# The first half of u's token contraction as filler inside attention, with w2 loaded early into the exp buffers and recalibrated scheduler costs

## Chip, cores, metric

One core of a Trainium2 chip runs the whole program. The metric is the device time of one execution in microseconds. Most executions of one kernel agree within about 1% here; each run also reports the mean granted clock of TensorE, as a share of full speed (0.972 in the profiled run of the kernel before). Engines: PE is TensorE, PEld its weight loads, DVE VectorE, ACT ScalarE, POOL GpSimd, SP SyncE.

## The reference

Four residual blocks on x (2048 tokens, 512 channels, bf16): attention, token-mixing MLP, and the same two again with the same weights.

```python
def _A_ref(x, wqkv, wo):            # 32 heads of 16, causal, window of 256 tokens
    q, k, v = ...
    scores = einsum(q, k) * Dh ** -0.5, masked
    return (softmax(scores) @ v) @ wo
def _B_ref(x, w1, b1, w2, b2):      # mixes tokens, not channels
    h = _layernorm(x)
    u = gelu(einsum("bsd,sf->bdf", h, w1) + b1)     # s = 2048 tokens, f = 1792
    return transpose(einsum("bdf,fs->bds", u, w2) + b2)
x = x + _A_ref(_layernorm(x)); x = x + _B_ref(_layernorm(x))
x = x + _A_ref(_layernorm(x)); x = x + _B_ref(_layernorm(x))
```

What matters: u contracts over tokens. Its first 8 token tiles are final when half of the query chunks of the attention are done, the last only at its end.

## The kernel before

A list scheduler on the host orders all operations of the five engines from estimated costs and latencies; the emitted program is static. On PE, scores come first ("sc"), then P·V or filler ("f": projections, output projection, y).

Shortened; "..." marks cuts, and the comments are mine.

```python
def op(self, eng, fn, ..., cost=100.0, lat=60.0, ...)     # lat=160 given for matmuls
...
w1b = sb("w1b", [P, 2, NT, 256]); w2b = sb("w2b", [P, 2, NFT, 256])    # NT = 16, NFT = 14
psum2 = Pool("psum2", 3)            # pairs of banks: scores, u
psum = Pool("psum", 2); psum.classes = {"od": [0, 1], "f": [0, 2]}     # P.V and fillers
...
def u_phase(w1t):
    last_sc = prev_sc[0]                              # the last scores of this attention
    ...
    for fb in range(NFT // 2):
        tu, tw = Tile(psum2), w1t[fb]
        for tt in range(2):
            for s0 in range(0, NT, 4):                # four token tiles at a time
                def f_u(e, ...): ...                  # 4 matmuls of 512 columns, PSUM accumulates over 16
                op("tensor", f_u, reads=[tw] + [f"xh{sc}" ...], writes=[(tu, tt)], after=[last_sc], cls="f")
        for tt in range(2):                           # gelu straight from PSUM
            op("scalar", lambda e: e.activation(uT[:, ft, :], PS[...], ACTF.Gelu_apprx_tanh, bias=b1col[...]))
...
for layer in range(2):
    prepare(0, True)                                  # layer 1: y blocks 0..3, layernorm, qkv
    for c in range(2 * NC):                           # eight query chunks
        tos[c] = attention(c, tqs, tks)               # scores, exp on ACT, mask on DVE, P.V
        if c == 5: late = [prev_sc[0]]
        if c % 2 == 0 and c // 2 + 1 < NC: prepare(c // 2 + 1, False)
        wo_block(c, tos[c], c == 2 * NC - 1)          # output projection, residual, layernorm
    w1t = [load_w1(fb, late) for fb in range(NFT // 2)]
    w2t = [load_w2(i, late) for i in range(NT // 2)]
    u_phase(w1t)
for t in range(NT): y_block(t, w2t, True); store(t)
```

The softmax here doesn't subtract the row's maximum and nothing guards it: scores larger than these inputs give would overflow.

## Time and profile before

The time is 563.89 us, median of three runs (563.68 to 564.19). The profiled run has a span of 560.8 us. I cut it into four stages. The borders are read from the times of the 304 exp instructions (152 per attention: 12 in the first query chunk, 20 in each other) and of the gelus in the trace. "Chunks" below count from 0.

| stage | before, us |
|---|---|
| A: start to the last exp of the first attention | 185.4 |
| B: from there to the last gelu | 59.1 |
| C: from there to the last exp of the second attention (y runs inside) | 207.2 |
| D: from there to the end (u again, then y) | 109.1 |

From the page of the kernel before: total busy times, then the busy share in tenths for 40 equal slices of 14.0 us, and last the granted clock in tenths.

```profile
PE 466.9 (83%) x7500; PEld 236.5 (42%) x7584; DVE 306.9 (55%) x659; ACT 342.4 (61%) x464; POOL 152.4 (27%) x266
...
PE   4967878877766969999888888999786596999997
...
ACT  0699999999988311110798997099979931120000
...
PEclk9999999999967989999999999999999998999999
```

ACT is at 9 through most of the first attention, then nearly idle in B, where PE is at 9: one engine after the other. PEclk is not at 9 in slices 11, 12 and 14, counted from 0, and once more near the end.

Stretches of the first attention in the kernel before; the columns are length, busy time with the number of instructions for each engine, granted clock, DMA share and GB/s.

```profile
core 0: us, PE busy (x) PEld busy (x) DVE busy (x) ACT busy (x) POOL busy (x), PEclk, DMA share, GB/s
91.00:147.00 56.00, 43.26 (x1154) 24.60 (x1157) 41.71 (x81) 54.96 (x74) 21.32 (x30) 1.00 0.20 52
147.00:157.00 10.00, 7.65 (x199) 3.83 (x199) 9.19 (x23) 9.45 (x14) 3.10 (x8) 1.00 0.50 123
157.00:167.40 10.40, 7.37 (x163) 3.99 (x164) 3.64 (x10) 9.80 (x14) 0.00 (x0) 0.51 0.01 2
167.40:174.30 6.90, 4.17 (x126) 2.05 (x128) 5.84 (x13) 5.67 (x9) 1.48 (x4) 0.99 0.01 2
174.30:184.50 10.20, 7.19 (x148) 4.03 (x150) 2.95 (x6) 8.60 (x13) 0.00 (x0) 0.50 0.02 4
```

Up to 147 us ACT is the bound (54.96 of 56.00) and PE has holes (43.26). From 157 us the clock is half for 10 us, full for 7, half again for 10.

The chain of waits of the kernel before in stage B: start, length, engine, what, line; L713 is u.

```profile
198.38 1.92 PE PS L713 x8
200.31 6.03 DMA w1b<-in_B_w_dram
206.38 5.88 PE PS L713 x14
212.31 10.74 PE PS L713 x49
```

Its PE timeline around the wait for a w1 block; the brackets hold the idle time and what ended it.

```profile
198.38 3.63 PE L713 MATMUL PS<-xh_sb,w1b 128*128 128x512 bf16 x16 [0.86 <-DVE xh_sb L468]
206.38 7.39 PE L713 MATMUL PS<-xh_sb,w1b 128*128 128x512 bf16 x20 [4.38 <-DMA w1b<-in_B_w_dram]
```

49 u matmuls take 10.74 us, 0.219 each (0.216 from start to start; the 10.74 hold the whole last one). After 4.38 us of idling for w1 the next 14 take 5.88 us (chain), 0.42 each: the half clock (0.50) stands in the trace for 6.8 us, from 205.0 us on. This is the "cold restart" below.

Groups of the kernel before that give durations for the additions of the change: line, engine, operation, operands, shapes, count | busy us, mean ns | idle before.

```profile
L681 DVE TENSOR_TENSOR x_sb<-x_sb,PS 128x512 bf16<-128x512 bf16 x32 | 21.8, 684 | 9.5 <-PE PS L678 9.4
...
L721 ACT ACTIVATE uT<-PS,b1col 128x512 bf16<-128x512 f32 x28 | 19.3, 688 | 83.0 <-PE PS L713 83.0
```

### The profile page before, as it was taken

To read this page: it belongs to the slowest core of one execution; us is meant where nothing else is said; L and a number is where in the kernel's file an instruction comes from. 1 tells how busy PE (TensorE), PEld (TensorE's weight loads), DVE (VectorE), ACT (ScalarE), POOL (GpSimd) and SP (SyncE) were. 2 spreads that over 40 slices of the span, in tenths; PEclk is the share of its full clock that TensorE was granted. 3 is DMA by queue.
4 is the path that set the end of the run, shared out by engine and by line. 5 is a ranking of instruction groups with operands and counts; after the bars stand their busy time and mean duration, and the time that the engine had idled before them with its cause. 6 is when DMAs were issued, how large, how long until landed. Compare 5 with 4: busy or idle time off the path is not lost.

```text
span 560.8 us, 16670 instructions
## 1 busy us (share of the span) xinstructions
PE 466.9 (83%) x7500; PEld 236.5 (42%) x7584; DVE 306.9 (55%) x659; ACT 342.4 (61%) x464; POOL 152.4 (27%) x266
## 2 busy tenths in 40 slices
PE   4967878877766969999888888999786596999997
PEld 1544444444433424445445444444444342444443
DVE  5998876886745300027866785876777630001222
ACT  0699999999988311110798997099979931120000
POOL 3874363252311000004516321651442100000000
PEclk9999999999967989999999999999999998999999
DMA  8221100002900062503312004301290005432653
GB/s 275 37 40 31 40 2 3 4 2 58 228 4 2 1 151 77 148 26 106 85 31 59 4 2 86 85 12 12 58 248 2 3 1 150 122 105 80 182 176 107
DMA packets 81367, 39.88 MB, mean 71 GB/s; under 512 B 17808, under 2 KB 81296, under 8 KB 81296
## 3 DMA queue, kind: packets, MB, share of 16 engines
q1 hardware_dynamic: 81296, 38.81, 26.7%
q8 instruction: 59, 0.97, 0.7%
q14 instruction: 12, 0.10, 0.1%
HBM read 33.56 MB, written 2.10 MB: 64 GB/s over the span
## 4 chain that ended last, share of the span: by engine, by line
PE 49%; ACT 20%; DVE 18%; POOL 5%; DMA 4%; issue 3%; POOLq 0%
ACT pt L621 18%; PE PS L713 16%; PE PS L728 15%; PE PS L647 7%; PE PS L526 4%; DVE stats L455 3%; DVE pt L631 3%; PE PS L607 3%; DVE xh_sb L468 2%; DMA w1b<-in_B_w_dram 2%; DVE x_sb L681 2%; POOL rstd L466 2%; PE PS L551 2%; DVE stg L560 2%; PE PS L678 1%
## 5 line engine op out<-in xcount | busy, mean ns | idle before, releaser
L621 ACT ACTIVATE pt<-PS 128x1024 bf16<-128x1024 f32 (+1 forms) x304 | 293.7, 1037 | 62.2 <-PE PS L607 62.1
L713 PE MATMUL PS<-xh_sb,w1b 128*128 128x512 bf16 x436 | 102.5, 392 | 11.5 <-DMA w1b<-in_B_w_dram 8.5
L728 PE MATMUL PS<-uT,w2b 128*128 128x512 bf16 x425 | 99.7, 379 | 6.1 <-issue 2.2
L647 PE MATMUL PS<-pt,vbd 128*32 128x64 bf16 (+3 forms) x1920 | 84.0, 240 | 19.6 <-DVE stg L560 5.3
L732 DVE SCALAR_TENSOR_TENSOR x_sb<-PS,b2col,x_sb 128x512 bf16<-128x512 f32 x32 | 24.0, 750 | 137.9 <-PE PS L728 137.8
L631 DVE TENSOR_TENSOR pt<-pt,ldm 128x512 bf16<-128x512 bf16 (+1 forms) x192 | 78.7, 413 | 34.8 <-ACT pt L621 33.4
L647 PE MATMUL PS<-pt,onesbd 128*32 128x64 bf16 (+3 forms) x1920 | 82.7, 238 | 0.8 <-issue 0.8
L607 PE MATMUL PS<-qT,kbd 32*128 32x64 bf16 (+3 forms) x1920 | 62.1, 236 | 18.8 <-ACT pt L621 17.3
L713 PEld LDWEIGHTS PS<-xh_sb,w1b 128*128 128x128 bf16 x448 | 44.2, 101 | 67.6 <-DMA w1b<-in_B_w_dram 9.5
L526 PE MATMUL PS<-xhT,wqkv 128*128 128x512 bf16 x227 | 61.5, 389 | 12.2 <-DVE stg L534 3.7
L721 ACT ACTIVATE uT<-PS,b1col 128x512 bf16<-128x512 f32 x28 | 19.3, 688 | 83.0 <-PE PS L713 83.0
L464 POOL TENSOR_SCALAR rstd<-agg 128x1 f32<-128x1 f32 x64 | 13.4, 209 | 206.8 <-DVE agg L457 205.2
L647 PEld LDWEIGHTS PS<-pt,vbd 128*32 128x32 bf16 x1920 | 45.1, 98 | 53.1 <-DVE oT L669 11.0
L537 POOL TENSOR_SCALAR kbd<-stg,par 128x512 bf16<-128x512 bf16 x64 | 51.6, 815 | 51.7 <-DVE stg L534 47.0
L728 PEld LDWEIGHTS PS<-uT,w2b 128*128 128x128 bf16 x448 | 41.0, 98 | 53.6 <-DVE x_sb L732 3.2
L563 POOL TENSOR_SCALAR vbd<-stg,half 128x512 bf16<-128x512 bf16 x64 | 49.4, 783 | 48.0 <-DVE stg L560 36.1
L607 PEld LDWEIGHTS PS<-qT,kbd 32*128 32x128 bf16 x1920 | 28.2, 94 | 66.7 <-ACT pt L621 44.8
L647 PEld LDWEIGHTS PS<-pt,onesbd 128*32 128x32 bf16 x1920 | 46.5, 99 | 1.2 <-issue 0.9
L455 DVE BATCH_NORM_STATS2 stats<-x_sb 128x6 f32<-128x512 bf16 x64 | 43.4, 683 | 0.9 <-DMA x_sb<-in_A_x_dram 0.3
L551 PE MATMUL PS<-wqkv,xhT 128*64 128x256 bf16 x512 | 35.3, 276 | 4.7 <-DVE stg L560 1.7
L466 POOL TENSOR_TENSOR rstd<-rstd,mhalf 128x1 f32<-128x1 f32 x64 | 37.3, 585 | 4.0
L664 ACT ACTIVATE rl<-PS 128x256 f32<-128x256 f32 x64 | 25.7, 401 | 20.0 <-PE PS L647 19.8
(36 smaller groups left out, 316.0 us busy)
## 6 DMA issues: line engine op xcount, KB each, us to landing
w1b<-in_B_w_dram SPq DMA_DIRECT2D x14, 1024.0 KB, 5.9
w2b<-in_B_w_dram SPq DMA_DIRECT2D x16, 896.0 KB, 5.4
out_dram<-x_sb SPq DMA_DIRECT2D x16, 128.0 KB, 2.2
wqkv<-in_A_wqkv_dram SPq DMA_DIRECT2D x3, 512.0 KB, 6.5
x_sb<-in_A_x_dram SPq DMA_DIRECT2D x3, 512.0 KB, 9.2
x_sb<-in_A_x_dram SPq DMA_DIRECT2D x2, 256.0 KB, 3.0
wo_sb<-in_A_wo_dram SPq DMA_DIRECT2D x1, 512.0 KB, 9.2
xhT<-xh_sb SPq DMA_TRANSPOSE x24, 2.5
```

The lines of the kernel that those rows point to most:

```text
L455: op("vector", lambda e: e.bn_stats(stats[:, t, :], x_sb[:, t, :]), reads=[f"x{t}"], writes=[f"st{t}"], cost=dve_cost(512))
L466: op("gpsimd", lambda e: e.tensor_tensor(rstd[:, t, :], rstd[:, t, :], mhalf[:], op=ALU.pow), reads=[f"rs{t}", "mhalf"], writes=[f"rs{t}"] ...
L526: mm_group(ft, 4, lambda e, c: e.matmul(bank(ft), lhsT=wqkv[:, c, which * 512 + o * P:which * 512 + (o + 1) * P], rhs=xhT[:, tx.slot, c, : ...
L537: op("gpsimd", lambda e, h=h: e.tensor_scalar(kbd[:, tk.slot, o, :, h, :], stg[:, ts.slot, :].rearrange("p (s n) -> p s n", n=64), par[:, ...
L551: last = e.matmul(bank(ft)[64 * hf:64 * hf + 64, sc * 256:(sc + 1) * 256], lhsT=xhT[:, tx.slot, c, tok:tok + 64], rhs=wqkv[:, c, 1024:1536 ...
L563: op("gpsimd", lambda e, h=h: e.tensor_scalar(vbd[:, tk.slot, 2 * sp:2 * sp + 2, :, 16 * h:16 * h + 16], stg[:, ts.slot, :].rearrange("p ( ...
L607: last = e.matmul(PS[:, 2 * tt[r // 2].slot + r % 2, base + c0 * 64:base + (c0 + n) * 64], lhsT=kbd[32 * r:32 * r + 32, tk.slot, o, jj, :, ...
L621: op("scalar", lambda e, ts=ts, tp=tp, i=i, cols=cols: e.activation(pt[:, tp.slot, 2 * i:2 * i + 2, 0:cols], PS[:, 2 * ts.slot:2 * ts.slot ...
L631: return e.tensor_tensor(v, v, msk.unsqueeze(1).to_broadcast([P, 4, w]), op=ALU.mult)
L647: last = e.matmul(bank(t)[32 * r:32 * r + 32, den * 256 + q0 * 64:den * 256 + (q0 + n) * 64], lhsT=onesbd[:] if den else vbd[:, tk.slot, j ...
L713: last = e.matmul(PS[:, 2 * tu.slot + tt, :], lhsT=w1b[:, tw.slot, sc, tt * P:(tt + 1) * P], rhs=xh_sb[:, sc, :], start=(sc == 0), stop=(s ...
L728: mm_group(ft, NFT, lambda e, fc: e.matmul(bank(ft), lhsT=w2b[:, tw.slot, fc, k * P:(k + 1) * P], rhs=uT[:, fc, :], start=(fc == 0), stop= ...
```

## The change

The intent: PE has holes while ACT computes exps (busy 43.26 of 56.00 us from 91 to 147), and ACT has little to do while PE computes u (busy 6.39 of 38.00 us from 206 to 244). So the token tiles 0 to 7 of u are contracted inside attention's second half as the lowest-ranked filler, and the f32 partial sums (28 KB per partition) lie in buffers that are free then: w2's and uT's. After attention only tiles 8 to 15 are contracted; DVE adds the partial sum into the small buffer of the softmax denominators, and ACT takes gelu from there. w1 is loaded in halves, into four buffers of half the size, and asked for two query chunks earlier. As w2's buffers are taken, the first three pairs of w2 go to the six exp buffers, which are free between the attentions. The scheduler's latencies and costs are recalibrated too.

```diff
+    LAT = {"tensor": 205.0, "vector": 125.0, "scalar": 155.0, "gpsimd": 95.0, "sync": 0.0}
     (replaces lat=60, and lat=160 for matmuls; DMA completion 1500 -> 1900; several costs of POOL and DVE)
-        w1b = sb("w1b", [P, 2, NT, 256])
-        w2b = sb("w2b", [P, 2, NFT, 256])
+        w1b = sb("w1b", [P, 4, NT // 2, 256])
+        w2b = sb("w2b", [P, 2, 4096])
...
+        def u_first(fb, tw):
+            for tt in range(2):
+                ft = filler(False)
+                dst, keys = uA(2 * fb + tt)               # f32 view of w2b or uT
+                mm_group(ft, 8, lambda e, sc, tt=tt, ft=ft: e.matmul(
+                    bank(ft), lhsT=w1b[:, tw.slot, sc, tt * P:(tt + 1) * P], rhs=xh_sb[:, sc, :],
+                    start=(sc == 0), stop=(sc == 7)), [tw] + [f"xh{sc}" for sc in range(8)],
+                    prio=1e9 + len(g.ops), after=g.users_of(keys))
+                op("vector", lambda e, dst=dst, ft=ft: e.tensor_copy(dst, bank(ft)), ...)
+        def u_second(fb, tw):
+            ...                                           # token tiles 8..15, after the last scores
+                op("vector", lambda e, ...: e.tensor_tensor(tmp(), PS[...], src, op=ALU.add), ...)
+                op("scalar", lambda e, ...: e.activation(uT[:, ft, :], tmp(), ACTF.Gelu_apprx_tanh, ...))
...
-                if c == 5:
+                if c == 3:
                     late = [prev_sc[0]]
...
+                if c == 4:
+                    for fb in range(NFT // 2):
+                        u_first(fb, load_w1(fb, 0, late))
...
+            w1t = [load_w1(fb, 1, late) for fb in range(NFT // 2)]
+            for i in range(3):
+                load_w2(i, [prev_sc[0]])                  # i < 3: into pt, two buffers for each pair
+            for fb in range(NFT // 2):
+                u_second(fb, w1t[fb])
+            load_w2(3, late)
+            load_w2(4, late)
```

More of the change, by code (lines that the diff above doesn't have):

```diff
@@ L53, in __init__, with op @@
         self.readers = {}
-    def op(self, eng, fn, reads=(), writes=(), cost=100.0, lat=60.0, prio=None, dma=False, after=(), holds=(),
+    def op(self, eng, fn, reads=(), writes=(), cost=100.0, lat=None, prio=None, dma=False, after=(), holds=(),
            cfg=None, cls=None):
         o = Op()
-        o.idx, o.eng, o.fn, o.cost, o.lat, o.dma = len(self.ops), eng, fn, cost, lat, dma
+        o.idx, o.eng, o.fn, o.cost, o.dma = len(self.ops), eng, fn, cost, dma
+        o.lat = self.LAT[eng] if lat is None else lat
         o.prio = prio
@@ L94, in op, with users_of @@
         return o
+    def users_of(self, keys):
+        return [o for k in keys for o in [self.last_w.get(k), *self.readers.get(k, ())] if o is not None]
     def _alloc_time(self, o):
@@ L187, in schedule @@
                 o.end = dma_free
-                o.done = dma_free + 1500.0
+                o.done = dma_free + 1900.0
             else:
@@ L295, in pool_cost @@
 def pool_cost(n, ptrs=0):
-    return 300 + n / 1.4 + 83 * ptrs
+    return 195 + n / 1.4 + 83 * ptrs
 def stepped(v, n, step):
@@ L386, in bass_interleave_layers__sliding_block__mixer_token_mlp__prompt_kernel @@
         p_kv, p_pt, p_rl, p_oT = Pool("kv", 3), Pool("pt", NPT), Pool("rl", 2), Pool("oT", 3)
-        p_w1, p_w2 = Pool("w1", 2), Pool("w2", 2)
+        p_w1 = Pool("w1", 4)
         op("gpsimd", lambda e: e.memset(ident[:], 1.0), writes=["ident"], cost=150)
@@ L464, in ln_block @@
             op("gpsimd", lambda e: e.tensor_scalar(rstd[:, t, :], agg[:, t, 1:2], a, b, op0=ALU.mult, op1=ALU.add),
-               reads=[f"ag{t}"], writes=[f"rs{t}"], cost=200, prio=-1e5)
+               reads=[f"ag{t}"], writes=[f"rs{t}"], cost=272, prio=-1e5)
             op("gpsimd", lambda e: e.tensor_tensor(rstd[:, t, :], rstd[:, t, :], mhalf[:], op=ALU.pow),
-               reads=[f"rs{t}", "mhalf"], writes=[f"rs{t}"], cost=350, prio=-1e5)
+               reads=[f"rs{t}", "mhalf"], writes=[f"rs{t}"], cost=520, prio=-1e5)
             op("vector", lambda e: e.tensor_scalar(xh_sb[:, t, :], x_sb[:, t, :], agg[:, t, 0:1], rstd[:, t, :],
@@ L492, in mm_group @@
                 rd = reads(k0, k1) if callable(reads) else reads
-                op("tensor", f, reads=rd, writes=[dst], cost=mm_cost(k1 - k0, cols), lat=160, prio=prio, holds=holds, after=after, cfg="f",
+                op("tensor", f, reads=rd, writes=[dst], cost=mm_cost(k1 - k0, cols), prio=prio, holds=holds, after=after, cfg="f",
                    cls="f")
@@ L514, in f_tr @@
                     return last
-                op("tensor", f_tr, reads=[f"xh{t}", "ident"], writes=[ft], cost=4 * 60, lat=160, prio=fprio(),
+                op("tensor", f_tr, reads=[f"xh{t}", "ident"], writes=[ft], cost=4 * 60, prio=fprio(),
                    holds=[tx], cfg="f", cls="f")
@@ L519, in qkv @@
                     bank(ft).bitcast(dt.bfloat16)[:, 0:512].rearrange("p (c n) -> p c n", c=4)),
-                   reads=[ft], writes=[(tx, i)], cost=dve_cost(512, psum=True), prio=-2e5)
+                   reads=[ft], writes=[(tx, i)], cost=dve_cost(512, 0.5, psum=True), prio=-2e5)
             XT = [(tx, i) for i in range(4)]
@@ L557, in f_v @@
                         return last
-                    op("tensor", f_v, reads=[(tx, sp), "w2"], writes=[ft], cost=mm_cost(4, 256), lat=160,
+                    op("tensor", f_v, reads=[(tx, sp), "w2"], writes=[ft], cost=mm_cost(4, 256),
                        prio=fprio(), holds=[ts, tk], cfg="v", cls="f")
@@ L617, in attention @@
                             rd += [(tk, "k", o, h) for h in range(2)]
-                    prev_sc[0] = op("tensor", f_sc, reads=rd, writes=[tA, tB], cost=cols / 2.4 + 15, lat=160,
+                    prev_sc[0] = op("tensor", f_sc, reads=rd, writes=[tA, tB], cost=cols / 2.4 + 15,
                                     prio=len(g.ops), after=[prev_sc[0]] if prev_sc[0] else [], cfg="sc", cls="sc")
@@ L634, in f_mask @@
                                                    op=ALU.mult)
-                        op("vector", f_mask, reads=keys + LD, writes=keys, cost=dve_cost(4 * n * nc_ * 64, 0.5) + 60)
+                        op("vector", f_mask, reads=keys + LD, writes=keys, cost=dve_cost(4 * n * nc_ * 64, 0.5))
                     for k, o, base in su:
@@ L657, in attention @@
                             rd += [(tk, "v", jj, h) for h in range(2)]
-                        op("tensor", f_pv, reads=keys + rd, writes=[od[o]], cost=plan[k][2] * 128 / 2.4 + 15, lat=160,
+                        op("tensor", f_pv, reads=keys + rd, writes=[od[o]], cost=plan[k][2] * 128 / 2.4 + 15,
                            holds=[to], prio=len(g.ops), cfg="pv", cls="pv")
@@ L686, in bass_interleave_layers__sliding_block__mixer_token_mlp__prompt_kernel, with load_w1 @@
         w2v = B_w2.rearrange("(fc p) s -> p fc s", p=P)
-        def load_w1(fb, late):
+        def load_w1(fb, hf, late):
             tw = Tile(p_w1)
-            op("sync", lambda e: e.dma_start(w1b[:, tw.slot], w1v[:, :, fb * 256:(fb + 1) * 256]), writes=[tw], dma=True,
-               cost=5000, prio=1e6 + len(g.ops), after=late)
+            op("sync", lambda e: e.dma_start(w1b[:, tw.slot], w1v[:, 8 * hf:8 * hf + 8, fb * 256:(fb + 1) * 256]),
+               writes=[tw], dma=True, cost=2500, prio=1e6 + len(g.ops), after=late)
@@ L692, in load_w1 @@
             return tw
+        w2keys = lambda i: [("w2b", 4 * (i % 2) + k) for k in range(4)]
         def load_w2(i, late):
-            tw = Tile(p_w2)
-            op("sync", lambda e: e.dma_start(w2b[:, tw.slot], w2v[:, :, i * 256:(i + 1) * 256]), writes=[tw], dma=True,
-               cost=4500, prio=1e6 + len(g.ops), after=late)
-            return tw
-        u_ops = []
-        def u_phase(w1t):
-            last_sc = prev_sc[0]
-            op("scalar", lambda e: e.preload_act_table_set("gelu_apprx_tanh_and_others"), writes=["acttab"], cost=1280)
-            for fb in range(NFT // 2):
-                tu, tw = Tile(psum2), w1t[fb]
-                prio = fprio()
-                for tt in range(2):
-                    for s0 in range(0, NT, 4):
-                        def f_u(e, s0=s0, tw=tw, tt=tt, tu=tu):
-                            last = None
-                            for sc in range(s0, s0 + 4):
-                                last = e.matmul(PS[:, 2 * tu.slot + tt, :], lhsT=w1b[:, tw.slot, sc, tt * P:(tt + 1) * P],
-                                                rhs=xh_sb[:, sc, :], start=(sc == 0), stop=(sc == NT - 1))
-                            return last
-                        u_op = op("tensor", f_u, reads=[tw] + [f"xh{sc}" for sc in range(s0, s0 + 4)], writes=[(tu, tt)],
-                           cost=mm_cost(4, 512), lat=160, prio=prio, after=[last_sc], cfg="f", cls="f")
-                        u_ops.append(u_op)
-                for tt in range(2):
-                    ft = 2 * fb + tt
-                    op("scalar", lambda e, ft=ft, tu=tu, tt=tt: e.activation(
-                        uT[:, ft, :], PS[:, 2 * tu.slot + tt, :], ACTF.Gelu_apprx_tanh, bias=b1col[:, ft:ft + 1], scale=1.0),
-                       reads=[(tu, tt), "b1", "acttab"], writes=[f"uT{ft}"], cost=act_cost(512, 1))
@@ L725, in y_block @@
-        def y_block(t, w2t, wide):
+            if i < 3:
+                halves = [Tile(p_pt), Tile(p_pt)]
+                for h, tw in enumerate(halves):
+                    op("sync", lambda e, h=h, tw=tw: e.dma_start(
+                        pt[:, tw.slot].rearrange("p a b -> p (a b)")[:, 0:NFT * 128].rearrange("p (f n) -> p f n", n=256),
+                        w2v[:, 7 * h:7 * h + 7, i * 256:(i + 1) * 256]), writes=[tw], dma=True, cost=2300,
+                       prio=1e6 + len(g.ops), after=late)
+                w2t[i] = ([[tw] for tw in halves], lambda fc: pt[:, halves[fc // 7].slot].rearrange(
+                    "p a b -> p (a b)")[:, (fc % 7) * 256:(fc % 7 + 1) * 256])
+                return
@@ new lines, in load_w2, with uA @@
+            op("sync", lambda e: e.dma_start(w2b[:, i % 2, 0:NFT * 256].rearrange("p (f n) -> p f n", n=256),
+                                             w2v[:, :, i * 256:(i + 1) * 256]), writes=w2keys(i), dma=True,
+               cost=4600, prio=1e6 + len(g.ops), after=late)
+            w2t[i] = ([w2keys(i)] * 2, lambda fc: w2b[:, i % 2, fc * 256:(fc + 1) * 256])
+        def uA(ft):
+            i = ft // 2
+            if ft % 2 == 0:
+                return (w2b[:].rearrange("p a b -> p (a b)").bitcast(dt.float32)[:, i * 512:(i + 1) * 512],
+                        [("w2b", i)])
+            return (uT[:].rearrange("p a b -> p (a b)").bitcast(dt.float32)[:, i * 512:(i + 1) * 512],
+                    [f"uT{2 * i}", f"uT{2 * i + 1}"])
@@ new lines, in bass_interleave_layers__sliding_block__mixer_token_mlp__prompt_kernel @@
+        u_ops, w2t = [], {}
+        def u_first(fb, tw):
[4 more added lines that the diff above has]
+                    bank(ft), lhsT=w1b[:, tw.slot, sc, tt * P:(tt + 1) * P], rhs=xh_sb[:, sc, :],
+                    start=(sc == 0), stop=(sc == 7)), [tw] + [f"xh{sc}" for sc in range(8)], prio=1e9 + len(g.ops),
+                    after=g.users_of(keys))
+                op("vector", lambda e, dst=dst, ft=ft: e.tensor_copy(dst, bank(ft)), reads=[ft], writes=keys,
+                   cost=dve_cost(512, psum=True), prio=-2e5)
@@ new lines, in u_second, with f_u @@
+        def u_second(fb, tw):
+            tu = Tile(psum2)
+            for s0, s1 in ((8, 12), (12, 14), (14, 16)):
+                for tt in range(2):
+                    def f_u(e, s0=s0, s1=s1, tt=tt):
+                        last = None
+                        for sc in range(s0, s1):
+                            last = e.matmul(PS[:, 2 * tu.slot + tt, :], lhsT=w1b[:, tw.slot, sc - 8, tt * P:(tt + 1) * P],
+                                            rhs=xh_sb[:, sc, :], start=(sc == 8), stop=(sc == NT - 1))
+                        return last
+                    u_ops.append(op("tensor", f_u, reads=[tw] + [f"xh{sc}" for sc in range(s0, s1)], writes=[(tu, tt)],
+                                    cost=mm_cost(s1 - s0, 512), prio=fprio(), after=[prev_sc[0]], cfg="f", cls="f"))
+            tmps = []
+            for tt in range(2):
+                src, keys = uA(2 * fb + tt)
+                tr = Tile(p_rl)
+                tmps.append((tr, lambda tr=tr: rl[:, tr.slot].rearrange("p a b -> p (a b)")))
+                op("vector", lambda e, tt=tt, src=src, tmp=tmps[tt][1]: e.tensor_tensor(
+                    tmp(), PS[:, 2 * tu.slot + tt, :], src, op=ALU.add),
+                   reads=[(tu, tt), "acttab"] + keys, writes=[tr], cost=dve_cost(512, psum=True))
+            for tt in range(2):
+                ft = 2 * fb + tt
+                tr, tmp = tmps[tt]
+                op("scalar", lambda e, ft=ft, tmp=tmp: e.activation(uT[:, ft, :], tmp(), ACTF.Gelu_apprx_tanh,
+                                                                    bias=b1col[:, ft:ft + 1], scale=1.0),
+                   reads=[tr, "b1", "acttab"], writes=[f"uT{ft}"], cost=act_cost(512, 1, psum=False))
@@ L726, in y_block @@
+        def y_block(t, wide):
+            if t % 2 == 0 and 8 <= t < NT - 2:
+                load_w2(t // 2 + 1, [])
             ft = filler(wide)
-            tw, k = w2t[t // 2], t % 2
+            k = t % 2
+            keys, w = w2t[t // 2]
             mm_group(ft, NFT, lambda e, fc: e.matmul(
-                bank(ft), lhsT=w2b[:, tw.slot, fc, k * P:(k + 1) * P], rhs=uT[:, fc, :],
+                bank(ft), lhsT=w(fc)[:, k * P:(k + 1) * P], rhs=uT[:, fc, :],
                 start=(fc == 0), stop=(fc == NFT - 1)),
-                lambda a, b: [tw] + [f"uT{fc}" for fc in range(a, b)], after=[u_ops[-8]])
+                lambda a, b: [q for h in range(a // 7, (b - 1) // 7 + 1) for q in keys[h]] +
+                             [f"uT{fc}" for fc in range(a, b)], after=u_ops[-6:-5])
@@ L736, in bass_interleave_layers__sliding_block__mixer_token_mlp__prompt_kernel @@
         out_v = out.rearrange("b (t p) d -> p (b t) d", p=P)
-        w2t = None
         for layer in range(2):
@@ L744, in prepare @@
                     if layer:
-                        y_block(t, w2t, wide)
+                        y_block(t, wide)
                     ln_block(t, False)
@@ L755, in bass_interleave_layers__sliding_block__mixer_token_mlp__prompt_kernel @@
                 wo_block(c, tos[c], c == 2 * NC - 1)
-            w1t = [load_w1(fb, late) for fb in range(NFT // 2)]
-            w2t = [load_w2(i, late) for i in range(NT // 2)]
-            u_phase(w1t)
+                if c == 4:
+                    for fb in range(NFT // 2):
+                        u_first(fb, load_w1(fb, 0, late))
+            op("scalar", lambda e: e.preload_act_table_set("gelu_apprx_tanh_and_others"), writes=["acttab"], cost=1280)
+            w1t = [load_w1(fb, 1, late) for fb in range(NFT // 2)]
[5 more added lines that the diff above has]
+            load_w2(4, late)
         for t in range(NT):
-            y_block(t, w2t, True)
+            y_block(t, True)
             op("sync", lambda e, t=t: e.dma_start(out_v[:, t, :], x_sb[:, t, :]), reads=[f"x{t}"], dma=True, cost=600,
```

## The prediction

> **What bounds it now** (slice table, stretch-by-stretch busy times; PE TensorE, ACT ScalarE, DVE VectorE).
> - Layer-1 attention is ACT-bound: in 91 to 147 us ACT is busy 55.0 of 56, PE 43.3. In 112 to 183, ACT 66.0 of 71, PE 51.6: 19 us of PE holes. From 154 to 182 the granted clock is only 0.50 to 0.95.
> - After each attention comes a serial PE tail, from the first u matmul to the last: 183.2 to 243.8 (60.6 us), 449.6 to 507.9 (58.4 us). The chain of waits there is almost only u matmuls: 224 at 0.219 us (49 in 10.74 us), 49.1 us. The rest is output projection, end of P·V, a 0.9 us wait for xh, a 4.4 or 4.2 us idle wait for a w1 load, and a slow restart: 14 matmuls in 5.88 us instead of 3.1 (4.56 in the second tail). [...]
> - y with layer-2 attention (244 to 413): PE 150 of 169; final y: 48 of 53, PE-bound.
>
> **What the change does.** PE's work stays. The instruction order shows only 56 (layer 1) and 44 (layer 2) of the 112 first-half u matmuls before attention's last output projection; 56 and 68 follow it and fill the wait for the last layernorm, where 40 u matmuls stood before anyway. From the last score matmuls on, the new tail holds 178 and 190 u matmuls, 39.1 and 41.7 us, plus 4 to 5 us of projection and P·V and 2 to 3 us of softmax latency: about 46 and 49 us against 61 and 59. The w1 wait and cold restart should vanish: first halves are loaded during attention, second halves in half-size loads. Gain about 15 + 10 = 25 us.
>
> Added: 28 DVE copies and 28 additions of 128x512 f32 (estimate 0.69 us each, from the 0.684 us of the PSUM copies and residual additions): 39 us. About half the copies fall in attention (DVE busy 47 of 71); the additions fall where DVE idles (0 busy in 206 to 244) and delay gelu by a microsecond. ACT and DMA bytes unchanged.
>
> **Given back.** 46 and 40 more matmuls (10 and 9 us) enter fragmented PE holes of 19 and 12 us; each pair delays a score matmul by up to 0.44 us. I expect 2 us lost per layer. The w2 prefetch fills all six exp buffers at the start of layer-2 attention and queues ahead of second-half w1 loads: 1 us. The recalibrated scheduler constants reorder everything; taken as neutral to slightly good.
>
> **Prediction: 542 us**, 8 in 10 within 533 to 553. Faster by over 2%: 0.88; within 2%: 0.11; slower: 0.01.
>
> **What would show it.**
> - From the last score matmuls to the last u matmul: 44 to 51 us per layer, without a w1 wait over 1 us.
> - Attention's second half (fourth to eighth query chunk) within 3 us per layer of before.
> - DVE busy up by 35 to 42 us; PE busy within 10 us.
> - y's first matmuls wait under 1.5 us for gelu.
>
> **What would make it wrong.** Filler delaying scores so that ACT loses over 3 us per layer; second-half w1 loads stuck behind the w2 prefetch; layer-2 exps waiting for buffers held by w2. On the other side, a fuller PE keeping the clock up from 154 to 189 us, or better constants removing small DVE waits, would bring it under 535.

(25 us gained, less 2 per layer and 1, make 20; 542 us lies 22 below the time.)

## More of the kernel before

Over the 10 us ahead of the first fall PE was busy 7.65, about as large a share as in the stretch up to 147 us. But in the last 3.4 us ahead of each of the two falls it was busy for only 1.89 and 1.23 us:

```profile
153.80:157.20 3.40, 1.89 (x75) 1.00 (x64) 3.37 (x10) 3.40 (x6) 1.62 (x4) 1.00 0.02 5
170.90:174.30 3.40, 1.23 (x52) 0.73 (x56) 2.73 (x8) 3.40 (x6) 1.39 (x4) 1.00 0.00 0
```

## The result, and the profile after

The changed kernel takes 527.13 us (median of four runs, 527.03 to 528.50) against 563.78 us (560.69 to 564.19) in the same series; the ratio is 0.9367, 95% interval 0.9330 to 0.9403. Ratios here are the mean of one kernel's fast runs over the mean of the other's in the same rounds, so not quite the ratio of the medians. The gain is 36.7 us; 22 were predicted, and 527 lies below the stated range of 533 to 553.

| stage | before | after | change | predicted change |
|---|---|---|---|---|
| A: to the last exp of the first attention | 185.4 | 178.5 | -6.9 | +2 |
| B: to the last gelu | 59.1 | 44.5 | -14.6 | -15 |
| C: to the last exp of the second attention | 207.2 | 203.6 | -3.6 | +3 |
| D: to the end | 109.1 | 98.7 | -10.4 | -10 |
| sum (profiled runs) | 560.8 | 525.3 | -35.5 | -20 |

(The prediction's figures are put to the stages here: the 1 us for the w2 prefetch is counted in C. They add up to 20 us, near the 22 that it took off the time.) B and D came as predicted. The surplus is in A, 8.9 us, and in C, 6.7.

C needs a closer look, which the times of the instructions in the traces allow. First, the last gelu comes later after the last u matmul than before, as the addition stands between them; measured to the first y matmul instead, B went from 58.0 to 41.8 us and C from 208.3 to 206.2, so about 1.6 us of C's surplus belong to B. Second, the second attention itself did not get shorter: from its first exp to its last it took 182.5 us before and 183.8 after. What shrank is the start of C, from the last gelu to the first exp, 24.7 us before and 19.7 after, with 70 y matmuls ahead of that exp instead of 80.

The same lines of the page, for the changed kernel; a slice is now 13.1 us.

```profile
PE 455.1 (87%) x7495; PEld 234.0 (45%) x7584; DVE 340.0 (65%) x715; ACT 340.1 (65%) x464; POOL 150.7 (29%) x266
...
PE   4977788878888899999988888999787889998997
...
ACT  0589999999999703403996997079999960231000
...
PEclk9989999999999999999999999999999999999999
```

PEclk shows one small dip at the start (half clock for 3.41 us, from 30.7 us on), and 9 from there on. DVE busy rose by 33 us.

Stretches of the changed kernel: chunk 6 to the last exp, and stage B in two parts.

```profile
core 0: us, PE busy (x) PEld busy (x) DVE busy (x) ACT busy (x) POOL busy (x), PEclk, DMA share, GB/s
137.40:178.50 41.10, 34.99 (x839) 18.19 (x846) 29.01 (x66) 41.10 (x57) 8.33 (x16) 1.00 0.13 36
178.50:202.00 23.50, 22.16 (x161) 10.69 (x163) 12.14 (x23) 3.45 (x7) 1.49 (x4) 1.00 0.84 224
202.00:223.00 21.00, 20.89 (x97) 9.51 (x97) 7.73 (x12) 8.28 (x13) 0.00 (x0) 1.00 0.42 121
```

From 137.4 to 178.5 us ACT is busy 41.10 of 41.10 us: no hole is left at the bound, with u filler on PE that was not there before. The same stretch of the kernel before, chunk 6 to the last exp:

```profile
138.50:185.40 46.90, 33.70 (x819) 18.35 (x820) 28.24 (x63) 42.55 (x57) 7.63 (x16) 0.78 0.33 82
```

It lasted 46.9 us, with ACT busy 42.55, at a mean clock of 0.78. So 5.8 of A's 6.9 us lie here. What ACT waited for from chunk 5 to the last exp (engine, line, releaser: us in total, times, longest), before and after:

```profile
ACT pt L621 <- PE PS L607: 3.0, 7, 1.2
ACT rl L664 <- PE PS L647: 1.9, 4, 0.8
```

```profile
ACT pt L628 <- PE PS L614: 0.5, 2, 0.3
ACT rl L671 <- PE PS L654: 0.2, 1, 0.2
```

The chain of waits of the changed kernel in stage B; L738 is the first half of u, L752 the second, L685 the output projection; the first line is the last of attention's work.

```profile
182.76 1.73 PE PS L685 x8
184.49 7.34 PE PS L738 x34
191.88 4.70 PE PS L738 x21
196.57 6.04 PE PS L752 x28
202.67 10.74 PE PS L752 x49
```

No wait for w1 and no cold stretch is left (the clock is 1.00 in both parts of stage B): 34 + 21 first-half matmuls cover the last layernorm, and the second half follows at 0.219 us each. The durations of the additions:

```profile
L768 ACT ACTIVATE uT<-rl,b1col 128x512 bf16<-128x512 f32 x28 | 18.7, 714 | 70.0 <-DVE rl L762 70.0
...
L762 DVE TENSOR_TENSOR rl<-PS,w2b 128x512 f32<-128x512 f32 x14 | 9.7, 692 | 31.5 <-PE PS L752 31.5
L742 DVE COPY w2b<-PS 128x512 f32<-128x512 f32 x14 | 9.7, 690 | 8.0 <-PE PS L738 8.0
```

They are as estimated: 0.69 us for a copy and for an addition. Gelu from SBUF takes 714 ns, from PSUM 688.

One odd thing is in the second layer's tail. PE timeline of the changed kernel there:

```profile
465.70 5.56 PE L752 MATMUL PS<-xh_sb,w1b 128*128 128x512 bf16 x25
471.10 5.34 PE L778 MATMUL PS<-uT,pt 128*128 128x512 bf16 x23
476.28 1.03 PE L738 MATMUL PS<-xh_sb,w1b 128*128 128x512 bf16 x4
478.82 8.38 PE L778 MATMUL PS<-uT,pt 128*128 128x512 bf16 x37 [1.51 <-DVE rl L762]
```

Four first-half matmuls (L738) run only after 23 matmuls of y (L778), and then PE waits 1.51 us for the addition that needed them. They rank below the second half and y. Below, they are called the straggler.

### The profile page after: what moved, and what is told of

The parts are those of the page before. It is cut to its first block, busy times and chain, and to the rows that moved or that the text cites. A ratio compares the mean times of both kernels' runs of the same rounds, so it can differ in the third digit from the quotient of the medians.

```text
span 525.3 us, 16776 instructions
## 1 busy us (share of the span) xinstructions
PE 455.1 (87%) x7495; PEld 234.0 (45%) x7584; DVE 340.0 (65%) x715; ACT 340.1 (65%) x464; POOL 150.7 (29%) x266
## 4 chain that ended last, share of the span: by engine, by line
PE 46%; ACT 34%; DVE 16%; issue 1%; DMA 1%; POOL 1%
ACT pt L628 30%; PE PS L778 16%; PE PS L752 9%; PE PS L738 7%; PE PS L654 5%; PE PS L533 3%; DVE stats L462 3%; PE PS L558 2%; DVE pt L638 2%; ACT rl L671 2%; PE PS L614 2%; DVE xh_sb L475 2%; DVE stg L567 2%; ACT rl L673 2%; PE PS L685 2%
## 5 line engine op out<-in xcount | busy, mean ns | idle before, releaser
L628 ACT ACTIVATE pt<-PS 128x1024 bf16<-128x1024 f32 (+1 forms) x304 | 297.9, 1075 | 60.3 <-PE PS L614 58.7
L654 PE MATMUL PS<-pt,vbd 128*32 128x64 bf16 (+3 forms) x1920 | 80.6, 235 | 13.5 <-DVE stg L541 5.1
L654 PE MATMUL PS<-pt,onesbd 128*32 128x64 bf16 (+3 forms) x1920 | 78.6, 233 | 0.0
L778 PE MATMUL PS<-uT,w2b 128*128 128x512 bf16 x263 | 61.6, 379 | 3.5 <-issue 2.1
L768 ACT ACTIVATE uT<-rl,b1col 128x512 bf16<-128x512 f32 x28 | 18.7, 714 | 70.0 <-DVE rl L762 70.0
L654 PEld LDWEIGHTS PS<-pt,vbd 128*32 128x32 bf16 x1920 | 44.5, 96 | 42.9 <-DVE oT L676 10.9
L544 POOL TENSOR_SCALAR kbd<-stg,par 128x512 bf16<-128x512 bf16 x64 | 49.7, 786 | 47.8 <-DVE stg L541 46.9
L738 PE MATMUL PS<-xh_sb,w1b 128*128 128x512 bf16 x209 | 50.1, 380 | 7.0 <-DVE w2b L742 2.4
L752 PE MATMUL PS<-xh_sb,w1b 128*128 128x512 bf16 x220 | 48.5, 379 | 0.2
L778 PE MATMUL PS<-uT,pt 128*128 128x512 bf16 x162 | 37.5, 379 | 2.6 <-DVE rl L762 1.5
L778 PEld LDWEIGHTS PS<-uT,w2b 128*128 128x128 bf16 x280 | 25.4, 98 | 32.0 <-DVE x_sb L688 0.9
L685 PE MATMUL PS<-wo_sb,oT 128*128 128x512 bf16 x112 | 30.5, 381 | 10.5 <-DVE x_sb L688 5.1
```

Of the source, the lines that this page charges most:

```text
L544: op("gpsimd", lambda e, h=h: e.tensor_scalar(kbd[:, tk.slot, o, :, h, :], stg[:, ts.slot, :].rearrange("p (s n) -> p s n", n=64), par[:, ...
L628: op("scalar", lambda e, ts=ts, tp=tp, i=i, cols=cols: e.activation(pt[:, tp.slot, 2 * i:2 * i + 2, 0:cols], PS[:, 2 * ts.slot:2 * ts.slot ...
L654: last = e.matmul(bank(t)[32 * r:32 * r + 32, den * 256 + q0 * 64:den * 256 + (q0 + n) * 64], lhsT=onesbd[:] if den else vbd[:, tk.slot, j ...
L738: mm_group(ft, 8, lambda e, sc, tt=tt, ft=ft: e.matmul(bank(ft), lhsT=w1b[:, tw.slot, sc, tt * P:(tt + 1) * P], rhs=xh_sb[:, sc, :], start ...
L752: last = e.matmul(PS[:, 2 * tu.slot + tt, :], lhsT=w1b[:, tw.slot, sc - 8, tt * P:(tt + 1) * P], rhs=xh_sb[:, sc, :], start=(sc == 8), sto ...
L778: mm_group(ft, NFT, lambda e, fc: e.matmul(bank(ft), lhsT=w(fc)[:, k * P:(k + 1) * P], rhs=uT[:, fc, :], start=(fc == 0), stop=(fc == NFT ...
```

## The experiments

Twelve runs. The question is why stages A and C, the attentions, became shorter although they took in more PE work. Theory A is that the recalibrated constants give better orders. Theory B is that the filler itself does it, by keeping the TensorE clock up where it had fallen. All kernels gave correct results. The first four ran together on one chip, the next four on a second, the last four on a third.

### e1_constants: only the constants

```diff
 kernel before
-    lat=60.0 (and lat=160 for matmuls), dma_free + 1500.0, 300 + n / 1.4, ...
+    LAT = {"tensor": 205.0, "vector": 125.0, ...}, dma_free + 1900.0, 195 + n / 1.4, ...   (all as in the change)
```

> The kernel before with only the scheduler's recalibrated latencies and costs; u, w1 and w2 as before. The open question is 15 us more gain than predicted, 10 of them in the second halves of the two attentions (5.5 and 4.1 us shorter although they took in 56 and 44 more matmuls). Theory A, the constants: about 553 us (551 to 556), the second halves (fourth chunk's end to the last exp) 5 and 4 us shorter, ACT without waits on scores there. Theory B, the filler matmuls themselves, which keep the TensorE clock at 1.0 from 154 to 189 us: 560 to 565 us, the clock still dips in that stretch, the second halves as before.

Measured: 549.82 us (547.39 to 554.04), ratio 0.9763 (0.9702 to 0.9823). That is more gain than either theory said (whether it exceeds 2% is unclear by the interval), and only partly where theory A put it: from chunk 4 to the last exp the first attention became 3.4 us shorter, the second 0.6 longer. Stages A to D changed by -4.6, -4.6, -2.5 and -3.4 us. Chunk 6 to the last exp became 43.3 us, and the clock there still falls, to a mean of 0.85.

The spread of the runs goes with the clock: 547.39 us at a mean clock of 0.984, 554.04 at 0.969. The tails shrink in part because the new order does the output projection in one piece and waits 5.3 us for w1 in place of 8.5.

### e2_structure: everything but the constants

```diff
 changed kernel
-    LAT = {"tensor": 205.0, "vector": 125.0, "scalar": 155.0, "gpsimd": 95.0, "sync": 0.0}, ...
+    LAT = {"tensor": 160.0, "vector": 60.0, "scalar": 60.0, "gpsimd": 60.0, "sync": 60.0}, ... (all as before)
```

> The changed kernel with the old latencies and costs in the scheduler. Theory A (constants): 536 to 540 us, the second halves of the attentions 4 to 5 us longer than in the changed kernel, ACT again waiting on scores. Theory B (filler keeps the clock up): 526 to 531 us, clock near 1.0 in the first attention's second half.

Measured: 527.62 us (527.24 to 527.69), ratio 0.9359: the same as the changed kernel. Theory A, as an explanation of the surplus in the total, falls here: with the structure in place the constants are worth nothing net. The stages differ, though. A is 180.8 us here (178.5 with the new constants), C is 206.2 (203.6), and D is 94.0 (98.7): the old constants put more u matmuls into the second attention and leave no straggler, which pays for the longer A and C. So within A and C the constants do have a part of the surplus, 2.3 and 2.6 us. Chunk 6 to the last exp has full clock with the old constants as well (1.00), and ACT is busy 41.47 of its 41.70 us.

### e3_dummy: only useless filler

```diff
 kernel before
                 wo_block(c, tos[c], c == 2 * NC - 1)
+                if c == 4 and layer == 0:
+                    for n in range(7):
+                        ft = filler(False)
+                        mm_group(ft, 8, lambda e, sc, ft=ft: e.matmul(
+                            bank(ft), lhsT=wo_sb[:, sc % 4, 0:P], rhs=xh_sb[:, sc, :], ...),   # never read
+                            ["wo"] + [f"xh{sc}" for sc in range(8)], prio=1e9 + len(g.ops))
```

> The kernel before with 56 useless 512-column matmuls (results never read, so outputs stay right) as lowest-priority filler in the second half of the first attention, at the places where the changed kernel does its u matmuls; everything else as before, old constants, and 12.3 us more PE work in all. Theory B: the granted clock stays near 1.0 there, that half is 3 to 6 us shorter, and the total falls to 556 to 561 us in spite of the added work. Theory A: no shorter, 564 to 568 us.

Measured: 553.82 us (552.83 to 555.97), ratio 0.9831 (0.9784 to 0.9877). With 56 matmuls that nobody reads, 12.3 us of PE work at 0.2195 us each, the program became about 10 us faster (faster beyond doubt, whether by 2% is unclear by the interval). The clock does not fall there (1.00), and chunk 6 to the last exp takes 42.3 us in place of 46.9:

```profile
139.40:181.70 42.30, 36.99 (x860) 19.81 (x871) 27.25 (x62) 41.43 (x57) 7.76 (x16) 1.00 0.37 92
```

Stage B shrank too, by 6.0 us. Eight of the useless matmuls stand where PE had waited for w1 (197.19 us), but the order of the useful instructions had moved too: the last output projection is done in one piece, as in e1. So this run alone does not separate work from order; e8_void does.

### e4_no_fill: the first half of u held back until attention is over

```diff
 changed kernel
-                    ..., prio=1e9 + len(g.ops), after=g.users_of(keys))
+                    ..., prio=fprio(), after=g.users_of(keys) + [prev_sc[0]])
-                if c == 4:
-                    for fb in range(NFT // 2):
-                        u_first(fb, load_w1(fb, 0, late))
+            w1f = [load_w1(fb, 0, late) for fb in range(NFT // 2)]       # after the last chunk
+            for fb in range(NFT // 2):
+                u_first(fb, w1f[fb])
```

> The changed kernel with the first half of u held back behind the last score matmuls of each attention, so that all 224 u matmuls per layer stand in the tail (178 and 190 in the changed kernel); copies, additions, buffers, w2 prefetch and constants stay. The moved matmuls are 46 and 34, 10.1 and 7.5 us at 0.2195 us. If filler in attention is free: 527 + 17.6 = 545 us. If it cost the 4 us that was predicted: 541 us. If theory B holds, attention without filler loses its clock and about 5 us more: 549 us or over. The w1 wait may come back in part, as the first-half loads free their buffers later.

Measured: 545.14 us (543.96 to 546.37), 18.0 us above the changed kernel's 527.13. The counts in the expectation don't hold: in the built program and in the trace, 40 and 30 first-half matmuls stand ahead of the last scores of the changed kernel, not 46 and 34. At 0.2195 us these are 15.4 us, not 17.6. So the overlap is worth 2.6 us more than the moved matmuls, and the filler costs attention nothing net. By stages, A is 2.5 us longer without the filler and C 0.4. Chunk 6 to the last exp takes 43.1 us, and the clock falls there again (mean 0.90), but the stretch is only 2.0 us longer than with filler, not 5; theory B, as I had sized it, was too strong.

Neither e4 nor the changed kernel waits for w1 at all; the new way of loading (halves, four buffers, asked for earlier) removes that wait even when all of u stands in the tail.

### e7_heat1 and e7_heat2: the order of before, with useless matmuls on the scores' path

```diff
 kernel before
                     def f_sc(e, su=su, tt=(tA, tB), hot=hot):
+                        for _ in range(hot):                 # 1 or 2 in chunks 5..7 of the first attention, else 0
+                            e.matmul(PS[:, 2 * tt[0].slot, :], lhsT=wo_sb[:, 0, 0:P], rhs=wo_sb[:, 1, :],
+                                     start=True, stop=True, skip_group_check=True)
```

> The kernel before with its instruction order kept on every engine; each of the 30 score groups in query chunks 5 to 7 of the first attention is preceded by one useless 512-column matmul into the bank that the scores then overwrite (6.6 us of added PE work, on the path of the scores). Theory B (a PE that is too idle loses its clock, and the lost clock costs ACT time): the granted clock dips less or not at all after 157 us, chunk 6's start to the last exp is 2 to 5 us shorter than the 46.9 us of before, total 556 to 561 us. Rival A' (the order of the filler, not the clock, shortened that stretch in the dummy run): no shorter or longer by up to 6 us, total 564 to 571 us.

> The same with two useless matmuls ahead of each of those 30 score groups (13.2 us added). Theory B: no dip of the clock between 110 and 185 us, chunk 6 to last exp 3 to 5 us shorter than before, total 555 to 560 us, unless the 0.44 us on each score group already starves ACT. Rival A': 566 to 577 us.

Measured: 570.16 us (ratio 1.0137) and 570.65 us (1.0141); theory B's expectations failed, and the totals lie where the rival A' had them. The kernels meant to hold the clock up without moving anything failed as a test of it, and I had misjudged where there is slack. (Of the 6.5 and 6.7 us by which the profiled runs are longer than that of before, 2.9 and 5.1 lie in A. C and D, where nothing was changed, are 4.5 and 3.2 us longer together; this is not explained.) In chunk 5, where the clock is full (1.00) in all three, 21.8 us became 23.2 and 24.7: each chunk has 10 score groups, so 2.2 and 4.4 us of added work cost 1.5 and 2.9 us. From chunk 5 to the last exp ACT waits 7.8 us for scores in e7_heat2, against 3.0 before.

Between 116.7 and 138 us of the kernel before, ACT was busy 20.90 of 21.30 us, and even so work added ahead of the scores there cost 1.5 and 2.9 us, while the filler of the changed kernel cost nothing net (e4_no_fill). The clock did stay up in e7_heat2:

```profile
141.50:190.50 49.00, 37.02 (x888) 18.39 (x897) 28.15 (x63) 42.77 (x57) 7.64 (x16) 1.00 0.31 78
```

Chunk 7 to the last exp took 24.4 us there against 24.7 before, in spite of the work that had cost chunk 5 2.9 us. That fits a clock worth some 3 us, but the two effects are mixed here.

### e8_void: the filler's places without its work

```diff
 e3_dummy
-                            bank(ft), lhsT=wo_sb[:, sc % 4, 0:P], rhs=xh_sb[:, sc, :], ...
+                            bank(ft)[:, 0:16], lhsT=wo_sb[:, sc % 4, 0:P], rhs=xh_sb[:, sc, 0:16], ...
```

> The dummy-filler kernel with every useless matmul cut from 512 columns to 16; the order of instructions is the same on every engine, so only the PE work of the 56 fillers is gone. If it was the clock that the filler kept up: the dips come back between 150 and 190 us, chunk 6's start to the last exp goes from 42.3 us back to 45 to 48, and the total, though 12 us of PE work lighter, is 557 to 565 us, slower than the 553.8 of the dummy filler. If it was the order: no dips matter, 545 to 554 us.

Measured: 558.41 us (557.38 to 559.48), ratio 0.9893. e3_dummy, run again beside it on the same chip as e9_dummy_again:

> The dummy-filler kernel once more, on the same chip as the one with the void fillers: 552 to 556 us again, no clock dip between 110 and 185 us.

Measured: 555.97 us (553.64 to 556.93), ratio 0.9846. The order of instructions is the same on every engine in both; only the columns of the useless matmuls differ. Chunk 6 to the last exp, first e9_dummy_again, then e8_void:

```profile
137.80:180.00 42.20, 36.96 (x860) 19.73 (x870) 27.22 (x62) 41.33 (x57) 7.80 (x16) 1.00 0.37 92
```

```profile
139.50:185.00 45.50, 33.01 (x863) 19.37 (x865) 27.16 (x62) 41.87 (x57) 7.80 (x16) 0.86 0.34 85
```

With the work the stretch has full clock and takes 42.2 us; without it the mean clock is 0.86 and it takes 45.5. So 3.3 us of that stretch come from the work of the filler alone, with the order fixed. What ACT waited for scores from chunk 5 to the last exp, in e3_dummy (the same kernel as e9_dummy_again) and in e8_void, shows where the time went:

```profile
ACT pt L621 <- PE PS L607: 0.8, 3, 0.4
```

```profile
ACT pt L621 <- PE PS L607: 2.7, 6, 1.4
```

Removing 12 us of PE work made the whole program slower, by 2.4 us in the medians, and the runs of the two kernels don't overlap. The rest of the way to the 46.9 us of before, 1.4 us, can be the order, or the clock that fell for longer there (0.78); that stays open.

The void kernel also corrects the reading of e3_dummy. It is itself 6.5 us faster than the kernel before on the same chip (558.41 against 564.87), with no work in its fillers: its stage B is 54.3 us, 4.8 shorter than before. So of the 8.9 us that the dummy filler gained on this chip, 2.4 are its work and the larger part is the order of the useful instructions that came with it.

### e6_order and e11_order_again: the straggler put first

```diff
 changed kernel, after the last chunk of each attention
+            for o in g.ops:
+                if o.prio is not None and o.prio >= 1e9:
+                    o.prio = 1e6 + len(g.ops) + (o.prio - 1e9) * 1e-5
```

> The changed kernel with one ranking changed: what is left of the first half of u after attention goes ahead of the second half of u and of y. In the changed kernel four of these matmuls of layer 2 ran only after 23 y matmuls, and y then stood 1.5 us waiting. From the last exp to the end the changed kernel takes 98.7 us, the one with the old constants, which has no such straggler, 94.0. Expected: 2 to 4.5 us less, 522.5 to 525.5 us; if the straggler is harmless: 527.

Measured: 525.72 us (525.08 to 526.48). From the last exp to the end 97.0 us in place of 98.7. The two kernels again, on one chip, with five rounds:

> The changed kernel, beside the reordered one on the same chip: 527 us.

> The changed kernel with the straggling first-half matmuls put first: 1 to 2 us (0.2 to 0.4%) below the changed kernel on the same chip, as the profiles say (523.3 against 525.3 us of span); if the earlier difference was one of chips, 527 as well.

Measured: changed kernel 527.34 us (526.80 to 527.77), reordered 525.80 us (525.31 to 526.91); the ratios to before are 0.9345 and 0.9321, and the intervals overlap. The small gain of 1.5 us appears on two chips and in the stage where the straggler stood, and is far below 2%. The intervals carry the spread of the kernel before; run against run, five of the six reordered runs lie below all six of the changed kernel. It has the lowest median.

### e5_w2_late: the w2 prefetch asked for later

```diff
 e6_order
-            for i in range(3):
-                load_w2(i, [prev_sc[0]])
             for fb in range(NFT // 2):
                 u_second(fb, w1t[fb])
+            for i in range(3):
+                load_w2(i, u_ops[-1:])
```

> That kernel again, with the w2 prefetch into the exp buffers undone in time only: the first three w2 pairs go to the same buffers, but are asked for after the last u matmul group. Each layer's y should then wait for a load: some 5 to 8 us idle PE (landing took 6.4 us for 448 KB, 5.3 for 896 KB) and a cold restart of about 3 us, so 8 to 11 us per layer, 539 to 547 us in total. If other work fills the wait: below 535 us.

Measured: 533.22 us (532.41 to 534.29), 7.5 us more than e6_order, on the same chip. That is less than expected: in the first layer PE waits nowhere for w2, because the scheduler begins with y blocks whose w2 lies elsewhere, at the price that the first exp of the second attention comes 7.3 us later after the last gelu. In the last stage PE does wait:

```profile
PE PS L778 <- DMA w2b<-in_B_w_dram: 4.6, 1, 4.6
```

So the prefetch is worth 7.5 us, and its queueing ahead of w1, which I had feared, costs nothing visible.

## Why the prediction was wrong

- **The tails: right.** From the last scores to the last u matmul the prediction had 61 to 46 us and 59 to 49. The traces have 61.4 to 44.4 and 59.0 to 52.9. The second lies outside the 44 to 51 that it named, because 23 y matmuls run ahead of the straggler; without it, it is 47.7 (e6_order). The w1 wait and the cold restart are gone. The counts behind it were a little off: 184 and 194 u matmuls stand behind the last scores, not 178 and 190.
- **The additions: right.** 0.69 us each, off the critical path. DVE busy rose by 33 us, just under the 35 to 42 predicted: the 56 records add up to 38.5 us, but busy time counts overlapping records once. y waits 1.5 us for gelu in the second layer only, because of the straggler.
- **"I expect 2 us lost per layer" and "1 us" for the prefetch: wrong, and in the first layer wrong in sign.** This is the failed step, the term "given back", with the fallen clock taken as given. The term sits in stages A and C, which were to grow by 5 us and shrank by 10.5. Two mistakes are in it. First, filler was charged with a delay of the scores. e4_no_fill shows that it costs nothing net: 18.0 us are lost without it, 15.4 by the count of the moved matmuls, and the first attention is 2.5 us longer. e7 shows that work on the scores' path did cost two thirds of itself in chunk 5, so what filler costs depends on where in PE's order it stands.
- **Second, I took the fallen clock from 154 to 182 us as given.** I had read it in the profile, and listed its removal only under what would bring the time below 535. From chunk 6 to the last exp of the first attention the change took 5.8 us off. With the order of every engine fixed, filler work held the clock at 1.0 and took 3.3 us off that stretch (e9_dummy_again against e8_void); with the new constants the filler was worth 2.0 there (e4_no_fill, 43.1, to the changed kernel, 41.1). The constants alone also shortened it, by 3.6 (e1_constants), but only by 0.6 once the structure was there (e2_structure, 41.7), so the 5.8 us can't be split cleanly. In the kernel before, the half clock stood twice for 10.2 us in a stretch in which PE's longest hole was 1.41 us.
- **"Attention's second half within 3 us per layer": missed.** From chunk 4 to the last exp it became 5.5 us shorter in the first layer and 5.0 in the second. In the second layer that is y work moved, not saved: 14 y matmuls fewer stand in it, and more in the first half.
- **"Recalibrated scheduler constants ... neutral to slightly good": right for the sum, wrong for the parts.** Without the structure they are worth 14 us (e1_constants), with it nothing net (e2_structure). The two gains overlap: each removes part of the same w1 wait and of the same fallen clock. In stage C the constants account for most of the change: -2.5 us in e1 and -3.2 in e4, -1.0 in e2, -3.6 in the changed kernel. It lies ahead of the first exp: from the first y matmul to that exp pass 22.4 to 22.6 us in the three kernels with the new constants (70 y matmuls ahead of it), 25.8 before and 25.3 in e2 (80 and 78). The -1.0 of e2 is hardly more than the spread: C took 206.8 to 209.9 us in the six profiles of kernels whose second layer is that of before.
- **PE busy within 10 us: missed narrowly**, 466.9 to 455.1. The work is the same; the likely reason is that at half clock the same matmuls are recorded longer (u matmuls 0.42 us each at a clock of 0.50, 0.219 at 1.00).

The runs of before support the part that the clock plays: in 25 of them the time goes from 560.3 us at a mean clock of 0.976 to 566.2 at 0.964 (correlation -0.75). The changed kernel runs at 0.994 to 1.0 and spreads over 1.7 us. A correlation alone would not show a cause; the pair with the fixed order does for its stretch.

## What to carry to other kernels

When a stage is bound by another engine, look at the TensorE clock in it before pricing extra matmuls there: PE work in the holes was free here (e4_no_fill) and even shortened a stretch, from 45.5 us at a mean clock of 0.86 to 42.2 at 1.00 with the order fixed (e8_void, e9_dummy_again). Price filler by where it stands: matmuls were free in the holes, and cost two thirds of themselves in front of the scores (1.5 of 2.2 us, 2.9 of 4.4). A filler also moves the useful instructions, so test it against a void one of the same order before crediting its work. And gains of two parts that remove the same wait don't add; run each part alone before crediting either.

## What the traces showed of the clock and the durations

- The granted clock. In the traces of the kernel before and the changed kernel, what lies between two changes of it lasts 3.41 us or a multiple of that (3.41, 6.83, 10.24 and so on). In the kernel before it falls to half five times, at 157.2, 174.3, 205.0, 471.3 and 560.0 us; in the step ahead of each fall PE was busy for a share of 0.56, 0.36, 0.12, 0.00 and 0.24. The changed kernel shows one fall, at 30.7 us, after a step of 0.44. Other steps of the kernel before with 0.50 to 0.56 (from 75.3, 430.3, 440.5 and 443.9 us) were not followed by a fall, so these traces give no sharp border. The first two falls came with no PE hole longer than 1.41 us from 110 to 185 us. PE's busy time is modelled, so the shares hold for such profiles only. With the filler's work a stretch took 42.2 us at a clock of 1.00, without it 45.5 at 0.86 (e9_dummy_again, e8_void).
- Matmuls of 512 columns in a row took 216 ns from start to start (median in the first tail of the kernel before, 212 to 243 us), with a weight load for every matmul.
- Matmuls without any use made a kernel faster: 558.41 us to 555.97 with the order of all instructions fixed (e8_void and e9_dummy_again).
- The f32 copies of 128x512 from PSUM took 690 ns each, the f32 additions from PSUM 692 and 682.
